# Moving high halves behind the next exponential, and four other steps, in a transformer block with adaptive LayerNorm

## The chip, the cores and the metric

The kernel runs on one core of one Trainium2 chip. The metric is the device time of one execution in microseconds; the time before is the median of three runs.

## The reference

One transformer block on 2048 tokens of 512 features, in float32. `c` is a vector of 512 numbers, from which six vectors of 512 follow (shift, scale and gate for each half of the block). The key and value caches are cut to their last 512 positions, without a mask; 32 query heads share 8 key heads of 128 features.

```python
mod = (_silu(c) @ w_mod).reshape(1, 6, 1, -1)          # sa, ca, ga, sb, cb, gb
h = layernorm(x) * (1 + ca) + sa
q = (h @ wq).reshape(1, 2048, 32, 128)                  # heads first
p = softmax(q @ k.T * 128 ** -0.5)                      # 512 keys
x = x + ga * ((p @ v) @ wo)                             # wo: 4096 x 512
h = layernorm(x) * (1 + cb) + sb
x = x + gb * ((gelu(h @ w_gate) * (h @ w_up)) @ w_down) # 512 x 1792 twice, 1792 x 512
```

## The kernel before

**Halves.** Each float32 operand of a matmul is split into a high half in float16 and a low half, the rest, also in float16. A product takes three matmuls of 128x128 by 128x512: high by low, high by high, low by high (`mm3`, L87 to L91). For scores the order is q's high half with K's low half, q's high with K's high, and then q's **low** half with K's high. `split_post` (L746 to L748) makes the halves of a product or of loaded weights: ScalarE (ACT) writes the high half, scaled, and a function that is returned writes the low half later on VectorE (DVE).

**Units and slots.** The attention has 128 units: a head and 512 tokens each. A unit has four slots of 128 tokens, so there are 512 slots (T = 512); unit u has slots 4u to 4u+3. A slot t issues, in this order (the loop begins at L1564): the scores of t on TensorE (PE) into one of two PSUM banks; the maximum `nm` of the row on DVE (L990); the entries noted for ("e", t), which are low halves of q and of outputs; the low half of p for slot t-3 on DVE (L1016) and its DMA transpose on SyncE (SP, L1020); the entries ("d", t), other work of DVE; the exponential of t on ACT (L999), which frees the scores' bank, and in odd slots the row sums' copy (L1004); the high half of p for slot t-2 on ACT (L1011); the entries ("x", t); then three products from a list (`pop`): q of the next unit, p times v of unit u-2, and the output projection; then loads, and the entries ("w", t). Nothing is reordered after that: each engine takes its instructions in the order in which the slots issue them. `at(key, fn)` notes an entry, `soon(fn)` notes it for ("d", now+1), `first(fn)` for ("e", now+1).

**The first three groups** (units 0 to 11) compute q directly (`q_plain`); from unit 12 on, 2x2 Strassen products with seven instead of eight blocks do it, two heads and 1024 tokens at a time. For unit u of the first kind q is complete after the second slot of the unit before, 4u-3, and `q_post` (L760) then issues its high half on ACT at once, ahead of the exponential of slot 4u-2; the low half follows in ("e", 4u-2). Weights of q for group 2 (`plain_steps`, L836 on) are split in slots 19 and 21, K of group 2 (`k_items`) in slot 24, each with its high half at the end of the slot and the low half in ("d", t+1).

**Combinations.** The Strassen products need sums of four blocks of LayerNorm output (b11, y, b22, b21), which lie in DRAM ("hs"). `combos` (L570 on) loads them ("cb") and issues differences on GpSimd (POOL, L582), high halves on ACT (L380) and low halves on POOL (L384). In the attention `sched_combos` (L1182 on) puts them at slots: for gen 1 from slots 201 and 234 on, for gen 2 (the feed-forward part of the first 1024 tokens) from 478 and 488 on. A load goes out `ahead` slots before the first use of its tile, 3 everywhere (`AHEAD`). The last ones (gen 3) are placed by hand in the feed-forward part by steps: step q is product q % 7 of group q // 7.

**LayerNorm of gen 2.** When the last projection of a tile of 128 tokens is added up (`attn_final`, L966 on), seven steps of its second LayerNorm are noted for later slots: statistics, normalising on POOL, the turn (four PE transposes into a PSUM bank `pln`, L508), two halves of scale and shift on ACT into `hf` (L516), after the second of which SP stores the tile to "hs", and two splits. Tiles 0 to 7 are concerned. PSUM banks "acc" are five in rotation, shared by q, p times v, projections, the turn and others.

**The feed-forward part** also uses Strassen products; the third product is transposed (`yt_tasks`, L1687) and DVE multiplies gate by up (L1294).

Of the kernel before, what the change touches and what calls it, by code (L numbers as in the profile page):

```python
# [26 lines left out]
QT = QB // P  # L27
EPS = 1e-5
SCALE = DH ** -0.5
AHEAD = 3  # L30
# [35 lines left out]
def block_kernel(ctx: ExitStack, tc: tile.TileContext, x, kT, v, wq, wo, wg, wu, wd, cT, wc, wm, out):  # L66
    nc = tc.nc
# [10 lines left out]
    def raw(name):  # L78
        return pool.tile([P, 512], F32, tag="raw", name=name, bufs=NRAW)
# [15 lines left out]
    def dma(out_, in_):  # L95
        moved[0] += 1
        nc.sync.dma_start(out_, in_)
# [81 lines left out]
    def col(name, i=0):  # L179
        return ST[name][:, i:i + 1]  # L180
# [193 lines left out]
    def stored(gen, name, p):  # L374
        qb, dt = {"b11": (0, p), "b21": (0, 2 + p), "y": (1, p), "b22": (1, 2 + p)}.get(name, (None, None))
        return spilled(gen, name)[:, p, :] if qb is None else spilled(gen, qb)[:, dt, :]

    def put(gen, name, p, src, eng):
        def high():
            nc.scalar.activation(block(gen, name)[:, p, :], src(), AF.Copy)  # L380

        def low():
            t = block(gen, name)
            eng.tensor_tensor(t[:, 2 + p, :], src(), t[:, p, :], op=ALU.subtract)  # L384

        return high, low
# [183 lines left out]
    def combos(gen, p, eng, base=True, d=0, e=0):  # L570
        X = {}

        def load(name):
            if gen == 0 and (p == 0 or name in ("b21", "b22")):
                X[name] = kept({"b11": "s1", "y": "u2", "b21": "u3"}[name]) if name != "b22" else \
                    pool.tile([P, 512], F32, tag="w2", name="cb", bufs=2)
            else:
                X[name] = raw("cb")
            dma(X[name], stored(gen, name, p))

        def diff(o, a, b):
            return lambda: nc.gpsimd.tensor_tensor(X[o], X[a], X[b], op=ALU.subtract)  # L582

        def parts(pos, name, tile_):
            high, low = put(gen, name, p, lambda: X[tile_], eng)
            return [(pos, high), (pos + 1 + e, low)]

        def plain(pos, name):
            return parts(pos, name, name) if base else []

        return [
            (lambda: load("b11"), plain(0, "b11") + [(2, diff("b11", "y", "b11"))] + parts(d + 4, "t1", "b11")),
            (lambda: load("y"), [(2, nop), (3, diff("y", "b22", "y"))] + parts(d + 5, "t3", "y")),
            (lambda: load("b22"), (plain(1, "b22") or [(2, nop)]) + [(4, diff("b22", "b22", "b11"))] + parts(d + 6, "t2", "b22")),
            (lambda: load("b21"), plain(3, "b21") + [(5, diff("b21", "b21", "b22"))] + parts(d + 7, "t4", "b21")),
        ]
# [15 lines left out]
    qT, pT, oT, E = {}, {}, {}, {}  # L612
# [3 lines left out]
    def sched(pos, ld, *more, kind="raw", ahead=AHEAD):  # L616
        loads.append(((pos,) + more, ld, kind, ahead))
# [10 lines left out]
    def get_qt():  # L628
        return pair("qt", "qt", 3)
# [106 lines left out]
    now = [0]  # L736
    later = {}

    def at(key, *fns):
        later.setdefault(key, []).extend(fns)  # L740
# [5 lines left out]
    def split_post(t, src, scale):  # L746
        nc.scalar.activation(t[:, 0, :], src, AF.Copy, scale=scale)  # L747
        return lambda: nc.vector.scalar_tensor_tensor(t[:, 1, :], src, scale, t[:, 0, :], op0=ALU.mult, op1=ALU.subtract)  # L748

    def soon(*fns):  # L750
        at(("d", now[0] + 1), *fns)

    def first(*fns):

        at(("e", now[0] + 1), *fns)

    def q_scale(u):
        return col("qsc", units[u][1])

    def q_post(u, ps):  # L760
        qT[u] = get_qt()
        first(split_post(qT[u], ps, q_scale(u)))

    def q_sum(u, t, ps, dst):
# [23 lines left out]
    SET, RAW = {}, {}  # L788
# [47 lines left out]
    def plain_steps(key, by):  # L836
        def part(k):
            SET.setdefault(key, [None, None])[k] = get_w(k)
            if key > 1:
                return soon(split_post(SET[key][k], RAW[key][k], by))  # L840
            times(RAW[key][k], by)
            halves(SET[key][k], RAW[key][k])

        return lambda: part(0), lambda: part(1)
# [50 lines left out]
    def kept(k):  # L895
        return pool.tile([P, QB], F32, tag=k, name=k, bufs=1)
# [69 lines left out]
    def attn_final(ti):  # L966
        y1[ti] = dram.tile([P, D], F32, name=f"y{ti}")
        dma(y1[ti], acc[ti])
        if ti < 2 * QT:
            nxt = ti + 2 * QT  # L970
            own, steps = ln_tile(2, ti, lambda: acc[ti])
            own()
            for d, fn in zip((1, 5, 8, 9, 10, 12, 13), steps):
                at(("w", now[0] + d), fn)
            at(now[0] + 12, lambda: load_acc(nxt, rows_of(x, nxt)))
        else:
            ln_last(ti - 2 * QT)
# [204 lines left out]
    def sched_combos(gen, p, base):  # L1182
        for k, (load, steps) in enumerate(combos(gen, p, nc.gpsimd if gen or p == 0 else nc.vector, False, 0 if gen else 1 if p else 2, 0 if gen or p else 5)):
            if gen == 0 and (p == 0 or k > 1):
                at(base + ((0, 0, 0, 2)[k] if p else (-10, -2, -1, -9)[k]), load)
                for off, fn in steps:
                    at(("w", base + off), fn)
            else:
                sched(base + steps[0][0], (load, [fn for _, fn in steps]), *[base + off for off, _ in steps[1:]])

    for p in range(2):
        sched_combos(0, p, CB[p])
# [25 lines left out]
    for g in range(NG):  # L1218
        half, pr = divmod(g, NPR)
        t0 = 16 * g  # L1220
        qd = pr // 2
        srcs = [wq[2 * pr], wq[2 * pr + 1]]
        by = col("wsc", pr)
        spread = None if half else lambda m, pr=pr: w_spread(pr, m)
        if 0 < g < GW:
            a, b = plain_steps(g, by)
            sched_pair(g, srcs, t0 - (19 if g > 1 else 13), spread, [(t0 - (13 if g > 1 else 8), a)], [(t0 - (11 if g > 1 else 7), b)])
        elif g >= GW and (not half or pr < GW):
            sched_set(g, srcs, t0, by, spread)
            if not half:  # L1230
                a, b, c, d, e, f = SETPOS2 if g == GW else SETPOS
                for k, pos in ((0, t0 - b + 4), (3, t0 - c + 4), (1, t0 - e + 4), (2, t0 - f + 4)):
                    at(pos, lambda g=g, k=k: store_set(g, k))
        elif half:
            for k, hi in ((0, 15), (1, 10), (2, 9), (3, 7)):
                within(t0 - 18, t0 - hi, lambda g=g, pr=pr, k=k: set_fetch(g, pr, k))
        if half:
            within(t0 - 14, t0 - 5, lambda pr=pr: k_fetch(pr))
            if pr % 2 == 0:
                within(t0 - 6, t0 + 3, lambda qd=qd: v_fetch(qd))  # L1240
                for k in range(4):
                    within(t0 + 4 + 2 * k, t0 + 22 + 2 * k, lambda h=4 * qd + k: wo_fetch(h))
        else:
            if g > 0:
                if pr % 2 == 0:
                    load, stat, spread_, parts = k_items(pr)
                    sched(t0 - (22 if g > 2 else 20), (load, [stat]))
                    at(("w", t0 - (19 if g > 2 else 17)), spread_)
                load, stat, spread_, parts = k_items(pr)
                sched(t0 - (7 if g > 2 else 8 if g > 1 else 6), (load, [parts if g != 2 else lambda parts=parts: soon(parts(True))]))  # L1250
                at(t0 - (3 if g > 2 else 1 if g > 1 else 2), lambda pr=pr: store(("k", pr), KV[0, pr, 0]))
                if pr % 2 == 0:
                    load, stat, spread_, parts = v_items(qd)
                    sched(t0 + 1, (load, [stat, spread_, parts]), t0 + 3, t0 + (6 if g > 2 else 5))
                    at(t0 + 10, lambda qd=qd: store(("v", qd), KV[0, qd, 1]))
            if pr % 2 == 0:
                wo_items(qd, [t0 + o + (qd == 7) for o in WOS[min(qd, 2)]], [t0 + o for o in WOP[min(qd, 2) + qd // 6]])
# [303 lines left out]
    with tc.manual_schedule():  # L1561
        begin()
        nexty, invs = [], {}
        for t in range(T + TAIL):  # L1564
            now[0] = t
            u, s = divmod(t, 4)
# [80 lines left out]
    def step(q, fn):  # L1647
        f_at(q // 7, q % 7, fn)

    for i, q in enumerate((16, 19, 22, 26, 30, 33, 36, 40)):  # L1650
        load, norm, split, turn = ln_turned(i)
# [3 lines left out]
        step(q + 4, turn)  # L1655
    for q, (qb, dt) in zip((37, 41, 44, 47, 50, 51, 54, 55), ((0, 0), (0, 2), (0, 1), (0, 3), (1, 0), (1, 2), (1, 1), (1, 3))):
        step(q, lambda qb=qb, dt=dt: turned_out(qb, dt))
    for p, (q, at_) in enumerate(((59, (61, 62, 62, 63, 64, 65, 66, 67, 68)), (70, (75, 76, 76, 79, 80, 81, 82, 89, 90)))):
        for load, steps in combos(3, p, nc.gpsimd):
            step(q, load)  # L1660
            for off, fn in steps:
                step(at_[off], fn)

    def whole(ti):
        if ti in halfway and ti in joined:
# [174 lines left out]
```

## Time and profile before

| | us |
|---|---|
| median of three runs (1731.09 to 1735.14) | 1733.09 |
| the profiled execution | 1734.19 |
| its span, first to last instruction | 1732.4 |
| TensorE busy | 1711.2 |
| VectorE busy | 1425.8 |
| ScalarE busy | 1254.3 |
| GpSimd busy | 1093.3 |

The profile is one execution. Its page gives the busy time of each engine and the costliest groups of instructions; other views of the same trace give waits (who waited for whom, us in total, times, longest), stretches of time, and the order of time: start, duration, engine, line, operation, output <- inputs, form, count, and in brackets the idle time of that engine before it with what ended it. A wait is put down to what came last by the profile, which need not be what was waited for. PE's instructions overlap: a row's end is later than the next row's start.

### The profile page before, as it was taken

How to read it: one execution, taken by the hardware profiler on the slowest of the kernel's cores; microseconds unless marked ns; L12 is line 12 of the kernel's file. 1: busy time of each engine (PE TensorE's matmuls, PEld its weight loads, DVE VectorE, ACT ScalarE, POOL GpSimd, SP SyncE). 2: the span in 40 equal slices, each digit the busy share in tenths (PEclk: the TensorE clock that was granted, in tenths of full speed). 3: DMA queues.
4: the chain of work that ended last, by engine and by line, in shares of the span. 5: the costliest groups of instructions: out<-in, count | busy, mean ns of one | idle time of the engine just before them, and what ended most of it. 6: DMA issues, size and time to landing. Idle time of an engine off the chain costs nothing.

```text
span 1732.4 us, 26343 instructions
## 1 busy us (share of the span) xinstructions
PE 1711.2 (99%) x8012; PEld 787.1 (45%) x8012; DVE 1425.8 (82%) x2476; ACT 1254.3 (72%) x2819; POOL 1093.3 (63%) x1328
## 2 busy tenths in 40 slices
PE   7999999999999999999999999999999999999998
PEld 5444444444444444444444444444444444444444
DVE  7888898988888899888888888888896788676666
ACT  6988788888888777897787777787785354455442
POOL 4879778777788884655665755747760345735424
PEclk9999999999999999999999999999999999999999
DMA  7999999999999998999999999999997556355353
GB/s 234 218 208 210 214 214 205 225 205 220 211 229 222 206 210 181 219 207 224 198 232 219 206 231 208 203 218 221 229 227 164 163 145 196 118 164 174 96 157 104
DMA packets 693454, 343.51 MB, mean 198 GB/s; under 512 B 579136, under 2 KB 602688, under 8 KB 693312
## 3 DMA queue, kind: packets, MB, share of 16 engines
q1 hardware_dynamic: 693024, 341.30, 85.4%
q8 instruction: 63, 1.03, 0.3%
q14 instruction: 79, 0.65, 0.1%
q10 hardware_dynamic: 288, 0.52, 0.1%
HBM read 137.50 MB, written 63.70 MB: 116 GB/s over the span
## 4 chain that ended last, share of the span: by engine, by line
PE 86%; DVE 5%; ACT 4%; POOL 2%; DMA 2%; issue 1%; SPq 0%; POOLq 0%; DVEq 0%; ACTq 0%
PE py L91 18%; PE po L91 17%; PE ps L91 16%; PE fa L91 8%; PE qa L91 8%; PE fc L91 4%; PE qc L91 4%; PE ya L91 3%; PE fb L91 2%; PE qb L91 2%; PE yc L91 2%; ACT ee L999 1%; DVE p L1016 1%; DVE nm L990 1%; ACT p L1011 1%
## 5 line engine op out<-in xcount | busy, mean ns | idle before, releaser
L999 ACT ACTIVATE ee<-ps,nm 128x512 f32<-128x512 f32 x512 | 349.6, 683 | 184.2 <-DVE nm L990 181.0
L1016 DVE SCALAR_TENSOR_TENSOR p<-ee,rr,p 128x512 f16<-128x512 f32 x512 | 454.1, 887 | 8.1 <-ACT p L1011 7.5
L990 DVE TENSOR_REDUCE nm<-ps 128x1 f32<-128x512 f32 x512 | 350.3, 684 | 105.7 <-PE ps L91 102.9
L91 PE MATMUL ps<-k,qt 128*128 128x512 f16 x1536 | 414.9, 379 | 3.8 <-ACT ee L999 2.5
L1011 ACT ACTIVATE p<-ee,rr 128x512 f16<-128x512 f32 x512 | 363.9, 711 | 21.9 <-DMA pt<-p 11.6
L91 PE MATMUL po<-pt,v 128*128 128x512 f16 x1536 | 372.9, 379 | 2.8 <-DVE kmax L184 1.0
L91 PE MATMUL py<-wo,ot 128*128 128x512 f16 x1536 | 371.3, 379 | 0.0
L91 PEld LDWEIGHTS <-w 128*128 128x128 f16 x2184 | 214.0, 98 | 259.7 <-issue 2.7
L91 PEld LDWEIGHTS <-v 128*128 128x128 f16 x1536 | 149.9, 98 | 185.1 <-issue 5.1
L91 PEld LDWEIGHTS <-ot 128*128 128x128 f16 x1536 | 150.3, 98 | 181.2
L91 PEld LDWEIGHTS <-qt 128*128 128x128 f16 x1536 | 145.8, 98 | 174.8 <-issue 3.3
L1320 POOL TENSOR_TENSOR fg<-fg 128x512 f32<-128x512 f32 x48 | 63.0, 1312 | 147.0 <-DVE fg L1294 144.2
L748 DVE SCALAR_TENSOR_TENSOR ot<-po,ot 128x512 f16<-128x512 f32 x128 | 87.8, 686 | 37.7 <-ACT ot L747 37.3
L1304 ACT ACTIVATE at<-fg 128x512 f16<-128x512 f32 x92 | 56.3, 626 | 80.1 <-DVE fg L1294 61.7
L999 ACT ACTIVATION_READ_ACCUMULATOR ee<-ps,nm 128x1 f32 x512 | 100.1, 195 | 0.0
L960 DVE SCALAR_TENSOR_TENSOR acc<-py,ysc,acc 128x512 f32<-128x512 f32 x128 | 94.7, 740 | 5.3 <-PE py L91 5.3
L91 PE MATMUL qa<-t,w 128*128 128x512 f16 x348 | 84.9, 379 | 0.0
L236 POOL TENSOR_TENSOR lw<-lw,half__86 128x1 f32<-128x1 f32 x39 | 25.0, 641 | 91.0 <-DVE lw L186 91.0
L91 PE MATMUL fa<-t,w 128*128 128x512 f16 x336 | 81.7, 379 | 0.1
L747 ACT ACTIVATE ot<-po 128x512 f16<-128x512 f32 x128 | 73.9, 577 | 5.0 <-PE po L91 5.0
L403 POOL TENSOR_TENSOR rs<-rs,nhalf 128x1 f32<-128x1 f32 x32 | 18.7, 586 | 92.9 <-DVE rs L397 90.0
L91 PEld LDWEIGHTS <-wo 128*128 128x128 f16 x504 | 49.3, 98 | 60.6 <-issue 1.3
(243 smaller groups left out, 2821.9 us busy)
## 6 DMA issues: line engine op xcount, KB each, us to landing
w<-kept SPq DMA_DIRECT2D x123, 256.0 KB, 3.3
wo<-kept SPq DMA_DIRECT2D x72, 256.0 KB, 3.3
kept<-stage SPq DMA_DIRECT2D x67, 256.0 KB, 3.2
raw<-in_wo SPq DMA_DIRECT2D x56, 256.0 KB, 3.2
kept<-w SPq DMA_DIRECT2D x39, 256.0 KB, 3.3
rw<-in_wq SPq DMA_DIRECT2D x38, 256.0 KB, 3.1
hs<-hf SPq DMA_DIRECT2D x32, 256.0 KB, 2.8
pt<-p SPq DMA_TRANSPOSE x512, 3.5
```

The source lines that it names most:

```text
L91: nc.tensor.matmul(ps, a, b, start=first and n == 0, stop=last and n == 2, skip_group_check=chain)
L236: nc.gpsimd.tensor_tensor(out, out, half_, op=ALU.pow)
L403: nc.gpsimd.tensor_tensor(st["rs"], st["rs"], nhalf, op=ALU.pow)
L747: nc.scalar.activation(t[:, 0, :], src, AF.Copy, scale=scale)
L748: return lambda: nc.vector.scalar_tensor_tensor(t[:, 1, :], src, scale, t[:, 0, :], op0=ALU.mult, op1=ALU.subtract)
L960: nc.vector.scalar_tensor_tensor(acc[ti], st["p"], by, acc[ti], op0=ALU.mult, op1=ALU.add)
L990: nc.vector.tensor_reduce(nm, E[t]["ps"], axis=AX.X, op=ALU.max, negate=True)
L999: nc.scalar.activation(e, E[t]["ps"], AF.Exp, bias=E[t]["nm"], scale=1.0, accum_out=sm[:, t % 2:t % 2 + 1])
L1011: nc.scalar.activation(p16[:, 0, :], E[t]["e"], AF.Copy, scale=E[t]["r"])
L1016: nc.vector.scalar_tensor_tensor(p16[:, 1, :], E[t]["e"], E[t]["r"], p16[:, 0, :], op0=ALU.mult, op1=ALU.subtract)
L1304: nc.scalar.activation(t[:, 0, :], g, AF.Copy)
L1320: nc.gpsimd.tensor_tensor(g[o], g[a], g[b], op=ALU.subtract)
```

## The change

Five edits. First, for units 3 to 7 the high half of q is issued one slot later, after that slot's exponential and high half of p, and its low half one slot later too. Second, the same for the weights of group 2 and for K of group 2. Third, the loads of combinations of gen 1 and gen 2 go out 3, 2, 1 and 3 slots ahead instead of 3 each: b11, y and b22 no longer in the same slot. Fourth, for tiles 3 and 7 the turn and the four steps after it come one slot later. Fifth, in the last combinations (second half of gen 3) the difference `y` goes from step 79 to 81, `b22` from 80 to 82, `b21` from 81 to 89, and the high and low halves that need them are spread over steps 83 to 96 (before: 81 to 90).

```diff
     def q_post(u, ps):
         qT[u] = get_qt()
+        if 2 < u < 8:
+            return at(("x", now[0] + 1), lambda: first(split_post(qT[u], ps, q_scale(u))))
         first(split_post(qT[u], ps, q_scale(u)))
...
             if key > 1:
-                return soon(split_post(SET[key][k], RAW[key][k], by))
+                return at(("x", now[0] + 1), lambda: soon(split_post(SET[key][k], RAW[key][k], by)))
...
-            for d, fn in zip((1, 5, 8, 9, 10, 12, 13), steps):
+            for d, fn in zip((1, 5, 9, 10, 11, 13, 14) if ti % QT == QT - 1 else (1, 5, 8, 9, 10, 12, 13), steps):
                 at(("w", now[0] + d), fn)
...
-                sched(base + steps[0][0], (load, [fn for _, fn in steps]), *[base + off for off, _ in steps[1:]])
+                sched(base + steps[0][0], (load, [fn for _, fn in steps]), *[base + off for off, _ in steps[1:]], ahead=(3, 2, 1, 3)[k] if gen else AHEAD)
...
-                sched(t0 - (7 if g > 2 else 8 if g > 1 else 6), (load, [parts if g != 2 else lambda parts=parts: soon(parts(True))]))
+                sched(t0 - (7 if g > 2 else 8 if g > 1 else 6), (load, [parts if g != 2 else lambda parts=parts: at(("x", now[0] + 1), lambda: soon(parts(True)))]))
...
-    for p, (q, at_) in enumerate(((59, (61, 62, 62, 63, 64, 65, 66, 67, 68)), (70, (75, 76, 76, 79, 80, 81, 82, 89, 90)))):
-        for load, steps in combos(3, p, nc.gpsimd):
-            step(q, load)
-            for off, fn in steps:
-                step(at_[off], fn)
+    for load, steps in combos(3, 0, nc.gpsimd):
+        step(59, load)
+        for off, fn in steps:
+            step((61, 62, 62, 63, 64, 65, 66, 67, 68)[off], fn)
+    for (load, steps), at_ in zip(combos(3, 1, nc.gpsimd), ((75, 76, 76, 80, 81), (76, 81, 83, 89), (76, 76, 82, 88, 89), (79, 80, 89, 95, 96))):
+        step(70, load)
+        for (_, fn), k in zip(steps, at_):
+            step(k, fn)
```

## Prediction

> **What bounds the kernel now.** I read the page first, then who waited for whom on PE, then the order of time around each wait.
>
> ```profile
> span 1732.4 us, 26343 instructions
> ...
> PE 1711.2 (99%) x8012; PEld 787.1 (45%) x8012; DVE 1425.8 (82%) x2476; ACT 1254.3 (72%) x2819; POOL 1093.3 (63%) x1328
> ...
> L91 PE MATMUL ps<-k,qt 128*128 128x512 f16 x1536 | 414.9, 379 | 3.8 <-ACT ee L999 2.5
> ```
>
> TensorE is busy for 99% of the span (the last row is one group: the scores, 379 ns each, 3.8 us of idle time before them), and no edit here removes or adds a matmul. So the change can only move the few places where PE stands still. In slots 15 to 31 of the attention this is its longest wait, by the view of waits cut to 62 to 98 us (total, times, longest):
>
> ```profile
> PE ps L91 <- ACT ee L999: 2.4, 3, 1.9
> ```
>
> The scores of a slot (ps) wait for the exponential two slots earlier, since there are two banks for scores. The longest, 1.9, is before the scores of slot 24. In order of time:
>
> ```profile
> 80.81 0.68 ACT L747 ACTIVATE qt<-pq,qsc 128x512 f16<-128x512 f32 x1
> 81.39 0.72 ACT L747 ACTIVATE w<-rw,wsc 128x512 f16<-128x512 f32 x1
> 81.53 0.75 DVE L748 SCALAR_TENSOR_TENSOR qt<-pq,qsc,qt 128x512 f16<-128x512 f32 x1 [0.98 <-ACT qt L747]
> 82.00 0.66 ACT L999 ACTIVATE ee<-ps,nm 128x512 f32<-128x512 f32 x1
> 82.66 0.69 ACT L1011 ACTIVATE p<-ee,rr 128x512 f16<-128x512 f32 x1
> 82.82 0.95 PE L91 MATMUL ps<-k,qt 128*128 128x512 f16 x3 [1.86 <-ACT ee L999]
> ```
>
> The exponential of slot 22 (82.00) stands on ACT behind the high half of q for unit 6 (80.81) and behind a high half of the weights (81.39). Both are what the first two edits move. After that wait the granted clock is low for one window (0.52, third from the right, in the table by stretches):
>
> ```profile
> 83.20:86.60 3.40, 3.40 (x10) 1.21 (x9) 3.40 (x7) 2.44 (x7) 3.22 (x4) 0.52 1.17 303
> ```
>
> At clock 0.52 this stretch lost 3.40 x 0.48 = 1.6 us of matmul time.
>
> **The change part by part.** Durations are from the profiled execution: 1734.19 us, span 1732.4, so 1.8 us around it.
>
> *High halves in slots 9 to 26.* No instruction is added. What is moved: for units 3 to 7 the high half of q goes from the end of slot 4u-3 to after the exponential **and** after the high half of p of slot 4u-2; the low half follows a slot later. But the scores of slot 4u need this q. So q's high half, which lay one slot ahead of need, becomes the last thing before them. Take unit 4:
>
> ```profile
> 62.39 0.68 ACT L747 ACTIVATE qt<-pq,qsc 128x512 f16<-128x512 f32 x1
> 62.96 0.63 ACT L219 ACTIVATE junk<-rw 128x512 f16<-128x512 f32 x1
> 63.58 0.66 ACT L999 ACTIVATE ee<-ps,nm 128x512 f32<-128x512 f32 x1
> ...
> 64.41 0.82 PE L91 MATMUL ps<-k,qt 128*128 128x512 f16 x3
> ```
>
> Now: q, statistics, exponential 14 until 64.24, scores of 16 at 64.41. After: all moves forward by q's 0.57 (62.39 to 62.96), but behind the exponential come the high half of p and that of q, 0.69 (row 82.66) and 0.68, or 0.6 each without the 0.1 by which such rows overlap. The scores can begin at 64.41 - 0.57 + 1.2 = 65.04. Their third matmul, 2 x 0.22 after the first (0.22 is (0.82 - 0.38) / 2, with the 0.38 of one alone), reads q's low half, 0.75 on DVE (row 81.53): it starts at 65.8 instead of 64.85, **0.95 later**. The same sum holds for units 5, 6 and 7. For slot 24 (unit 6) the exponential comes earlier by q and the weights ahead of it (0.58 + 0.61), and then p's and q's halves come behind it, 1.2: nothing gained there either.
>
> These delays don't add up, though, because ACT is the pace here: PE waits for it three times anyway, 2.4 us in all, and a delay of PE before slot 24 comes off the 1.86 us there. What ACT itself stood still is the bound of any gain. The two rows are the waits of ACT from 60 to 98 us and the busy time of PE, weight loads, DVE, ACT and POOL there:
>
> ```profile
> ACT ee L999 <- DVE nm L990: 1.9, 3, 0.9
> ...
> 60.00:98.00 38.00, 34.67 (x151) 14.94 (x152) 32.91 (x59) 35.58 (x88) 29.69 (x37) 0.96 1.03 221
> ```
>
> ACT is busy for 35.58 of the 38 us, longer than PE. What stays is what happens at the last deferred q, unit 7, after which PE sets the pace again:
>
> ```profile
> 88.11 0.72 ACT L747 ACTIVATE k<-raw,ksc 128x512 f16<-128x512 f32 x1
> 90.82 0.68 ACT L747 ACTIVATE qt<-pq,qsc 128x512 f16<-128x512 f32 x1
> 91.39 0.66 ACT L999 ACTIVATE ee<-ps,nm 128x512 f32<-128x512 f32 x1
> ...
> 90.61 0.68 DVE L990 TENSOR_REDUCE nm<-ps 128x1 f32<-128x512 f32 x1
> 91.53 0.75 DVE L748 SCALAR_TENSOR_TENSOR qt<-pq,qsc,qt 128x512 f16<-128x512 f32 x1 [0.24 <-ACT qt L747]
> ...
> 91.63 1.46 PE L91 MATMUL ps<-k,qt 128*128 128x512 f16 x6
> 97.06 0.59 PE L91 MATMUL po<-pt,v 128*128 128x512 f16 x2 [0.61 <-DVE nm L990]
> ```
>
> The six matmuls at 91.63 are slots 27 and 28 without a gap; slot 28 begins at 92.28. Also, since exponential 26 ends at 92.05, it could not have begun earlier: so the 1.6 us of slow clock before it cost this kernel at most 0.2 us, and nothing is won where it goes. After: K's high half (0.72) leaves slot 24 and lands before exponential 26, q's leaves that place; nm of slot 26 is ready at 91.29; the exponential stays at about 91.3 to 91.9, p's half until 92.6, q until 93.2, the third matmul 0.75 later at 94.0 instead of 92.85: 1.15 late. Against that the product po waits 0.61 at 97.06. I read this as the transposed p of slot 23, whose low half now no longer stands behind q's low half on DVE (0.75, row 91.53): the wait goes. Net **+0.5**. Bounds: everything that ACT and po waited comes back, -1.9 - 0.6 = -2.5; four delays in full, 4 x 1.05 = +4.2. I take +0.5, since it follows from rows at the place where PE takes over the pace. The weights' own move costs nothing: they are first read in slot 28, K in slot 32, and their low halves end by about 87 and 93; if that cover were gone, it would be their 0.75 on DVE once each. The raw tiles that the low halves free are loaded anew only some us later. On DVE the low half of p, and so its transpose, is queued behind each low half that waits.
>
> *Combination loads.*
>
> ```profile
> 535.92 1.48 SPq L97 DMA_DIRECT2D cb<-hs  x3
> 537.49 1.49 SPq L1020 DMA_TRANSPOSE pt<-p  x1
> 540.28 3.52 SPq L1020 DMA_TRANSPOSE pt<-p  x1
> ...
> 547.28 1.89 PE L91 MATMUL po<-pt,v 128*128 128x512 f16 x8 [1.01 <-DVE kmax L184]
> ```
>
> Three loads of 256 KB go out in one slot ahead of two transposes; the second of them needs 3.52 us to be issued, and po then waits 1.01. After, the second load is issued one slot and the third two slots later, behind one transpose each, so the third no longer stands before the transpose at 540.28. POOL takes each tile two slots after its new issue, some 5 us; if that were too little, POOL's differences would wait, and no matmul of these slots reads them. I take **-1.0**; between 0 (wait only moved) and -1.0. The other three groups of such loads (slots 233, 477, 487) lie where the view of PE's waits shows none: 0.
>
> *LayerNorm turn of tiles 3 and 7.*
>
> ```profile
> 730.70 0.80 ACT L516 ACTIVATE hf<-pln,cols 128x128 f32<-128x128 f32 x2
> 731.65 0.52 PE L508 MATMUL pln<-ident,acc 128*128 128x128 f32 x3 [0.63 <-POOL w L159]
> 774.51 0.63 PE L508 MATMUL pln<-ident,acc 128*128 128x128 f32 x4 [0.32 <-ACT hf L516]
> ```
>
> The view names POOL for the first, but the bank is what the tile before freed at 731.50, when its last hf ended. One slot later the bank is long free: **-0.63** for tile 3; its store on SP passes one transpose, and no wait of PE follows for 40 us. For tile 7 the 0.32 goes too, but every later step of that tile moves with it, its store on SP among them:
>
> ```profile
> 784.63 0.55 SPq L97 DMA_DIRECT2D hs<-hf  x1
> 789.49 0.36 SPq L97 DMA_DIRECT2D rw<-in_wu  x1
> 789.90 0.52 SPq L97 DMA_DIRECT2D kept<-stage  x1
> 790.53 1.32 SPq L1020 DMA_TRANSPOSE pt<-p  x1
> ...
> 794.47 1.89 PE L91 MATMUL po<-pt,v 128*128 128x512 f16 x8 [0.55 <-DMA pt<-p]
> ```
>
> One slot on, the store of 784.63 stands behind the next transpose and behind that slot's load and store (789.49, 789.90), right ahead of the transpose at 790.53, for which po waits. The load at 789.49 waits for a tile that POOL frees, so it comes no earlier. The transpose moves by the store's 0.55 and the 0.32 is waited for here instead: **+0.55** on this stretch, between -0.32 (the store is hidden) and +0.9 (its transfer delays the transpose's as well).
>
> *Last combinations.*
>
> ```profile
> 1485.00 2.61 POOL L582 TENSOR_TENSOR cb<-cb 128x512 f32<-128x512 f32 x2
> 1486.36 1.81 DVE L1294 SCALAR_TENSOR_TENSOR fg<-fg,gsc,fu 128x512 f32<-128x512 f32 x1
> 1493.76 0.81 DVE L1294 SCALAR_TENSOR_TENSOR fg<-fg,gsc,u 128x512 f32<-128x512 f32 x1
> 1489.53 0.81 PE L91 MATMUL ya<-at,wo 128*128 128x512 f16 x3 [0.77 <-DVE yt L1687]
> ```
>
> Beside POOL's two differences the DVE product takes 1.81 us; its like at 1493.76 takes 0.81. The two differences go two steps later, so the product ends some 1.0 us sooner, and with it the addition yt, for whose bank ya waits: the 0.77 goes: **-0.77**. No DMA is moved here. The same POOL work comes at steps 81 to 96, ahead of the first use at step 98: between -0.77 and, if one such product is slowed there in turn, +0.2.
>
> Sum: 0.5 - 1.0 - 0.63 + 0.55 - 0.77 = **-1.35**, hence 1732.85 for such an execution. The profiled one lay 1.10 above the median of the runs, 1733.09; taken from that median, **1731.7**.
>
> **The rivals.**
>
> *The slots gain as meant.* ACT makes good all that it waited: -2.5 in place of +0.5, the others as they are with tile 7 at 0: -2.5 - 1.0 - 0.63 - 0.77 = -4.9, **1728.2**. For it: the one long wait names ACT, and the two rows ahead of its exponential are the ones that go. Against: ACT is full there; moving work within a full engine frees none of it.
>
> *The wait for q takes the place of the wait for the exponential, in all four units* (slots 16, 20, 24, 28). That is slower than before. Price 4.2, and one stretch at half clock more, 1.6; less 1.85 for the other three parts: +3.95, **1737.0**. It decides on whether ACT runs on while PE waits: if the maxima that ACT needs come late because the scores came late, each delay is carried on.
>
> *Only the clock.* The new wait before slot 28 is about 1.6 us with two matmuls and then half a us more, like the one that brought 0.52 at 83.20; this time no wait of ACT's follows that would swallow the loss. +1.6: **1733.3**. [...]
>
> *The change doesn't do what it says*: the waits at 547, 731 and 1489 only turn up a little later. Then +0.5 alone: **1733.6**.
>
> **How the numbers follow.** Forecast 0.42 (1731.7, give or take 1.5), gain as meant 0.22, clock 0.14, nothing 0.08, q in all units 0.14. A measurement of this kernel can tell about 0.2%, 3.5 us, from no change: faster means under 1729.6, slower above 1736.6. Faster: most of the second case and a little of the first, 0.24. Slower: most of the last, 0.12. Same: 0.64. The range takes in the second case down to 1727.5 and the bounds of the first and the clock's case up to 1736.0; outside lies the last case and a little below, under 0.2.
>
> **What would show it.** Right: scores of slots 16, 20, 24 and 28 waiting for "ACT qt" or "DVE qt" in place of "ACT ee"; no wait of po near 547, of pln near 731 and of ya near 1489; po near 794 waiting longer for its transpose. Wrong: scores of slot 24 or 28 beginning earlier against the slots before them than now, or new waits of PE beyond slot 32 in the attention.

## The result and the profile after

The changed kernel takes 1735.63 us (median of 22 runs, 1733.86 to 1737.38), the kernel before 1733.01 (22 runs): a ratio of 1.0015, 95% interval 1.0009 to 1.0021. So it is slower, by 2.6 us, where 1.35 us less was forecast. The profiled execution took 1736.34 us, against 1734.19 before. One of the 11 executions of the kernel without the slots' edits, further below, took 7384 us; it moves the median there by less than 0.1.

The page of the changed kernel, first lines and the group of the scores:

```profile
span 1734.6 us, 26346 instructions
...
PE 1710.8 (99%) x8010; PEld 786.4 (45%) x8012; DVE 1422.2 (82%) x2476; ACT 1254.4 (72%) x2819; POOL 1094.3 (63%) x1328
...
L91 PE MATMUL ps<-k,qt 128*128 128x512 f16 x1536 | 415.9, 379 | 8.8 <-ACT qt L747 5.6
```

The work is the same; what grew is idle time ahead of the scores, 3.8 to 8.8 us, and q is now its main cause. To place the loss I set the start of each slot's scores beside its start in the trace of before (each start counted from the first instruction of its trace). After minus before, in us:

| slot (time before) | 30 (98) | 207 (549) | 280 (735) | 283 (743) | 296 (778) | 303 (796) | 511 | last matmul |
|---|---|---|---|---|---|---|---|---|
| late by | +1.47 | +1.14 | +0.31 | +0.85 | +0.34 | +3.52 | +2.94 | +2.14 |

The steps between the columns belong to one edit each: the high halves +1.5; the loads -0.3; tile 3's turn -0.8, then +0.5 at tile 4; tile 7's turn -0.5 for its own bank, then +3.2; the last combinations -0.9 (between 511 and the end, where smaller steps of both signs come to +0.1). The -0.6 between slots 303 and 511 is of no edit: most of it, at slots 459 to 462, is there with q's move alone too. The loss is made in two places.

**Slots 15 to 31.** Waits of PE from 62 to 98 us in the changed kernel (total, times, longest):

```profile
PE ps L91 <- ACT qt L747: 4.4, 4, 1.4
PE po L91 <- DVE p L1018: 1.0, 1, 1.0
PE ps L91 <- DVE qt L748: 0.7, 4, 0.2
```

The four waits for q are those that were foretold, and no wait for the exponential is left. The second row was not foretold. In order of time:

```profile
85.34 0.74 DVE L1018 SCALAR_TENSOR_TENSOR p<-ee,rr,p 128x512 f16<-128x512 f32 x1
...
86.00 1.70 DVE L748 SCALAR_TENSOR_TENSOR w<-rw,wsc,w 128x512 f16<-128x512 f32 x1
86.61 0.81 PE L91 MATMUL ps<-k,qt 128*128 128x512 f16 x3
87.24 0.94 POOL L159 TENSOR_SCALAR wo<-wor 128x512 f16<-128x512 f32 x1
87.63 0.68 DVE L992 TENSOR_REDUCE nm<-ps 128x1 f32<-128x512 f32 x1
88.34 0.66 ACT L1001 ACTIVATE ee<-ps,nm 128x512 f32<-128x512 f32 x1 [1.54 <-DVE nm L992]
89.08 1.46 PE L91 MATMUL po<-pt,v 128*128 128x512 f16 x6 [1.00 <-DVE p L1018]
```

A low half of the weights, 1.70 us on DVE (86.00), now stands ahead of a maximum, that of slot 24 (87.63). Behind that maximum the exponential waits 1.54 on ACT, and the transposed p comes 1.00 late for po.

**Tile 7.** Waits of PE from 722 to 800 us:

```profile
PE ps L91 <- ACT ee L1001: 2.0, 1, 2.0
PE pln L508 <- ACT hf L516: 0.3, 1, 0.3
```

Neither the old wait of pln at 774 nor that of po at 794 is there. The first row is new, and it is ACT's, not SP's:

```profile
777.80 3.80 POOL L1381 TENSOR_TENSOR rw<-rw 128x256 f32<-128x256 f32 x4
...
785.65 0.67 POOL L530 TENSOR_TENSOR b<-hf,b 128x256 f16<-128x256 f32 x1
...
780.18 0.71 ACT L1013 ACTIVATE p<-ee,rr 128x512 f16<-128x512 f32 x1
786.35 0.81 ACT L516 ACTIVATE hf<-pln,cols 128x128 f32<-128x128 f32 x2 [5.46 <-POOL b L530]
787.05 0.68 ACT L1001 ACTIVATE ee<-ps,nm 128x512 f32<-128x512 f32 x1
...
787.88 0.81 PE L91 MATMUL ps<-k,qt 128*128 128x512 f16 x3 [2.04 <-ACT ee L1001]
788.52 3.77 PE L91 MATMUL po<-pt,v 128*128 128x512 f16 x9
```

ACT stands still for 5.46 us at its first write of tile 7's `hf`, with exponentials queued behind it, until POOL's last read of tile 6's `hf` (785.65). That read waits its turn on POOL behind eight microseconds of other work. Then nine matmuls take 3.77 us. Two stretches with the granted clock (third column from the right):

```profile
784.00:788.00 4.00, 1.96 (x10) 0.83 (x9) 0.62 (x1) 1.62 (x6) 2.23 (x3) 1.00 0.80 181
788.00:792.00 4.00, 4.00 (x12) 1.45 (x11) 2.67 (x5) 3.83 (x10) 0.00 (x0) 0.60 0.77 178
```

The cause lies in the buffers. `hf` is taken from `raw`, five buffers (L78), which it shares with the staging of the feed-forward weights (`stage`). Which of the five a request gets stands in the addresses of the built programs. In the kernel before, tile 7's `hf` has the buffer that tile 5's had; in the changed kernel it has the very buffer of tile 6's, and its first write waits for POOL's read of that. The order of the requests is the same in both: tile 7's comes right after tile 6's. But one slot later it comes behind the issue of tile 6's last read on POOL, in the same slot 296; before, it came in slot 295, ahead of that read. With tile 7's turn alone moved, the addresses change in this way; with tile 3's alone they don't. By which rule the build picks a buffer is not shown here.

### The profile page after: what moved, and what is told of

Same layout as the page of the kernel before. It is cut to its first block, busy times and chain, and to the rows that moved or that the text cites. A ratio compares the mean times of both kernels' runs of the same rounds, so it can differ in the third digit from the quotient of the medians.

```text
span 1734.6 us, 26346 instructions
## 1 busy us (share of the span) xinstructions
PE 1710.8 (99%) x8010; PEld 786.4 (45%) x8012; DVE 1422.2 (82%) x2476; ACT 1254.4 (72%) x2819; POOL 1094.3 (63%) x1328
## 4 chain that ended last, share of the span: by engine, by line
PE 90%; DVE 3%; ACT 2%; POOL 2%; DMA 1%; issue 1%; SPq 0%; POOLq 0%; ACTq 0%; DVEq 0%
PE py L91 19%; PE po L91 18%; PE ps L91 17%; PE fa L91 8%; PE qa L91 8%; PE fc L91 4%; PE qc L91 4%; PE ya L91 3%; PE fb L91 2%; PE qb L91 2%; PE yc L91 2%; PE pq L91 1%; PE yb L91 1%; DVE nm L992 1%; ACT ee L1001 1%
```

## The experiments

My theory after the two traces: the slots lose because of the weights' low half on DVE besides the foretold half microsecond for q, and tile 7 loses because of the buffer that it gets from `raw`; the other edits gain. The rivals: q's waits carry the whole of the slots' loss; tile 7's wait belongs to SP or to what came before it. All times are medians of 11 runs, beside runs of the kernel before on the same chip; the ratio is taken over all of them and is not that of the two medians.

| kernel | us | before there | ratio, 95% interval |
|---|---|---|---|
| slots alone | 1735.07 | 1733.29 | 1.0008, 1.0 to 1.0017 |
| q alone | 1732.95 | 1733.29 | 0.9997, 0.9988 to 1.0006 |
| q and K | 1733.25 | 1733.38 | 1.0001, 0.9992 to 1.001 |
| weights alone | 1732.95 | 1733.38 | 0.9997, 0.9988 to 1.0006 |
| loads alone | 1732.54 | 1733.38 | 0.9995, 0.9986 to 1.0004 |
| turns alone | 1734.9 | 1733.38 | 1.0008, 0.9999 to 1.0017 |
| last combinations alone | 1733.04 | 1733.38 | 0.9998, 0.9989 to 1.0006 |
| all but the slots | 1734.09 | 1733.29 | 1.0003, 0.9994 to 1.0012 |
| all, own buffer for tile 7 | 1732.5 | 1733.29 | 0.9995, 0.9987 to 1.0004 |
| mended | 1730.2 | 1733.38 | 0.9983, 0.9974 to 0.9992 |
| mended, tile 4 later too | 1729.95 | 1733.38 | 0.9981, 0.9972 to 0.9989 |

Most single intervals take in 1, and each reaches about 1.5 us to either side, so the places and sizes below are read from the traces, one execution of each kernel. The medians agree with them, but can't prove them: slots +1.8, turns +1.5, loads -0.8, last combinations -0.3 make +2.2, beside the 2.6 measured for all.

**The slots: all three, all but the three, q alone.** The first has the edits of `q_post`, of the weights and of K on the kernel before; the second is the changed kernel without these; the third has only this:

```diff
     def q_post(u, ps):
         qT[u] = get_qt()
+        if 2 < u < 8:
+            return at(("x", now[0] + 1), lambda: first(split_post(qT[u], ps, q_scale(u))))
```

> The kernel before with the first two edits alone (high halves of q, of the weights and of K one slot later). Theory A (the loss has two sources, the slots and the turn of tile 7): the scores of slots 16, 20, 24 and 28 wait for q as in the changed kernel, the product of slot 25 waits 1.0 us for DVE, PE is 1.5 us late at slot 30 and stays so: 1734.5 us, +1.5 on before. Rival B (the slots carry the whole loss): +2.6 or more, 1735.6. Rival C (the slots cost nothing in the end): 1733.0.

> The changed kernel with the first two edits undone: loads, LayerNorm turns and last combinations are as changed. Theory A: PE is where it was in before at slot 30, loses 2.7 us between slots 295 and 303, gains 0.3 at slot 206, 0.3 at slots 278 to 283 and 0.9 in the last combinations: about +1.2 on before, 1734.1 us. Rival B (the loss is all in the slots): 1731 to 1731.5.

> The kernel before with the deferral of q alone; weights and K as before. Theory A (of the slots' loss about 1 us is the weights' low half, which on DVE came ahead of the maxima of slot 24, and 0.5 the wait for q before slot 28): the waits for q at slots 16, 20, 24, 28 are there, no wait of PE for DVE before slot 26, PE about 0.5 late at slot 30: 1733.5 us. Rival B (q's waits carry the slots' whole loss): PE 1.5 late at slot 30, 1734.5.

Measured: with all three, slot 30 is 1.35 late where slot 0 was 0.20 early, so the slots cost 1.55. With q alone slot 30 is 0.10 late and slot 0 0.34 early: 0.44, with the same four waits and without the wait of po at 97.06. That is the +0.5 of the prediction, for q. About 1.1 remains for weights and K. Without all three, slot 30 stands where it stood in before (0.03 late against slot 0), and the time is 1734.09, as the theory has it: the slots carry part of the loss, not the whole.

**Which of the two, and alone or together.** `qk_only` leaves the weights where they were; `w_only` moves nothing else:

```diff
             if key > 1:
-                return soon(split_post(SET[key][k], RAW[key][k], by))
+                return at(("x", now[0] + 1), lambda: soon(split_post(SET[key][k], RAW[key][k], by)))
```

> The kernel before with the moves of q's and K's high halves alone; the weights' stand where they stood. Theory (the weights' low half on DVE, moved ahead of the maxima of slot 24, is the part of the slots' cost that q alone does not bring): scores of slot 30 about 0.45 us late against before, as in the kernel with q's move alone, no wait of about 1.0 us of the product po for DVE in slot 25 or 26; span like that kernel's, about 1731.7, time about 1733.5. Rival (K's move brings it): scores of slot 30 about 1.5 us late and the wait of po there, span 1733.2.

> The kernel before with the move of the weights' high halves alone. Theory (a low half of the weights, 1.2 to 1.7 us on DVE beside POOL, falls ahead of the maxima of slot 24 once it is a slot later, whether q moves or not): the product po of slot 25 or 26 waits for DVE and slot 30 is 0.5 to 1.1 us late; about 1734. Rival (it costs only where q's waits have pushed everything back): slot 30 level with before or, with the high half out of the exponential's way before slot 24, up to 0.6 earlier.

Waits of PE from 62 to 98 us, first with q and K moved, then with the weights alone:

```profile
PE ps L91 <- ACT qt L747: 3.8, 4, 1.3
PE ps L91 <- DVE qt L748: 0.7, 4, 0.2
```

```profile
PE ps L91 <- ACT ee L999: 2.1, 3, 1.3
PE po L91 <- DVE p L1016: 1.2, 1, 1.2
PE po L91 <- DVE nm L990: 0.7, 1, 0.7
```

Without the weights' move there is no wait of po for DVE: that wait is theirs. Slot 30 then is 0.53 late and slot 0 0.29 early, 0.82 in all, 0.4 more than with q alone. This 0.4 is not K's. It is there at slot 16 already (1.29 late against slot 0, with q alone 0.89), and K's halves are moved in slot 24. It comes in at slot 14, where kernels that have no edit so early differ as well: the one with the turns alone loses 0.46 there on before, the one with the last combinations alone gains 0.21. From slot 16 to slot 30, q and K together win back 0.47 and q alone 0.45, while with the weights too 0.66 is lost, and 0.69 in the changed kernel. So K costs nothing, as the theory had it, and the weights 1.1. But with the weights alone the wait of po is there, 1.2 us, and slot 30 is 0.47 **early**, slot 0 0.18 early: a gain of 0.3. The rival of that run was right. Moving the weights also shortens the wait ahead of the scores of slot 24, 1.86 before and 1.32 here, and what po loses is made good by slot 30. Behind q's delays it is all loss; that this is because the scores of slot 24 are late there already is how I read it, not shown. So the 1.1 is an effect of the two edits together, not of either.

**Tile 7: a buffer of its own; the turns alone.**

```diff
-                st["f"] = raw("hf") if gen == 2 else tmp("hf")
+                st["f"] = pool.tile([P, 512], F32, tag="hf7", name="hf", bufs=1) if gen == 2 and qb and i == QT - 1 else raw("hf") if gen == 2 else tmp("hf")
```

> The changed kernel, with a buffer of its own for tile 7's hf, which otherwise takes the fifth buffer after tile 6's in the raw rotation. Theory A (ACT's hf waits 5.46 us until POOL has read tile 6's hf from the buffer that tile 7 is to get, and PE waits 2.0 us for the exponential behind it, then runs a window at half clock): ACT's wait, PE's wait before slot 299 and the half clock go, PE gains about 2.7 us between slots 295 and 303: 1732.9 us. Rival B (the store of tile 7 ahead of a transpose on SP, as I predicted, is what costs): PE still waits near 790 to 797, for the transpose, and gains less than 0.5: 1735.2 or more.

> The kernel before with the later turn of tiles 3 and 7 alone. Theory: tile 3 -0.8 near 732 and +0.5 near 743, tile 7 -0.5 for its own wait and then the wait of about 2.0 for the exponential near 788 that its hf brings: between +1.3 and, with the clock at half behind that wait, +3.0; about 1735. Rival (the wait for hf only came with another edit): no wait of PE near 788, 0.6 less than before.

One thing in the first of these is not so: tile 7 has tile 6's buffer, but not because it comes fifth after it in a rotation (see above).

With the changed kernel otherwise as it is, the buffer takes away ACT's wait, PE's wait and the low clock. ACT's first write of tile 7's `hf`, and the two stretches:

```profile
781.30 0.80 ACT L516 ACTIVATE hf<-pln,cols 128x128 f32<-128x128 f32 x2
...
784.00:788.00 4.00, 4.00 (x20) 1.85 (x19) 3.50 (x6) 3.37 (x9) 3.20 (x4) 1.00 0.79 186
788.00:792.00 4.00, 4.00 (x20) 1.77 (x19) 3.89 (x7) 3.97 (x12) 0.67 (x1) 1.00 1.23 234
```

From slot 296 to slot 303 it gains 0.70 on before where the changed kernel loses 3.18, and the time falls from 2.6 us above the kernel before to 0.8 below it. The store on SP, the only cost the prediction had here, has no effect: the view of PE's waits from 722 to 800 has a single row, that of pln at tile 4. The turns alone bring the same wait without any other edit, with the clock full behind it (waits and a stretch of that kernel):

```profile
786.28 0.81 PE L91 MATMUL ps<-k,qt 128*128 128x512 f16 x3 [1.99 <-ACT ee L999]
```

```profile
788.00:792.00 4.00, 3.96 (x19) 1.76 (x18) 3.84 (x8) 3.80 (x10) 0.00 (x0) 1.00 0.67 155
```

There slots 296 to 303 lose 1.64, in the kernel without the slots' edits 1.67; so the low clock made up some 1.5 of the 3.18 in the profiled execution of the changed kernel (3.18 less the 1.65 without it). How often it falls in its other executions the runs don't say.

**Loads alone.** The edit of `sched_combos` on the kernel before, nothing else.

> The kernel before with the changed lead of the combination loads alone. Theory: the wait of po near 547 us (1.01 before) goes, down to between nothing and 0.66, and nothing else of PE changes: 0.4 to 1.1 us less than before, about 1732.5. Rival (the wait is only moved to where the later loads stand ahead of a transpose): PE is level with before by slot 212, 1733.2.

PE has no wait at all from 530 to 560 us; slot 207 is 1.34 early, slot 0 0.14 early: a gain of 1.2, as foretold. In the trace of the changed kernel 0.66 of the wait stays, though its loads have the same leads. Its SP queue, and POOL:

```profile
538.00 1.28 SPq L1022 DMA_TRANSPOSE pt<-p  x1
539.33 2.33 SPq L97 DMA_DIRECT2D cb<-hs  x2
...
545.12 2.34 SPq L1022 DMA_TRANSPOSE pt<-p  x1
...
546.71 1.32 POOL L582 TENSOR_TENSOR cb<-cb 128x512 f32<-128x512 f32 x1 [2.94 <-DMA cb<-hs]
...
548.40 2.12 PE L91 MATMUL po<-pt,v 128*128 128x512 f16 x9 [0.66 <-DMA pt<-p]
```

Two things here are not as the prediction has them. The first load does not stay in its slot: the planner behind `sched_combos` lets loads out in the order of their uses, so b11 with its lead of 3 is queued behind y with its lead of 2, and the two go out together (x2), a slot later. And POOL's difference then waits 2.94 for its data. But the 0.66 belongs to this one execution. The kernel with tile 7's own buffer has the same instructions up to there; in its trace the like of the transpose at 545.12 takes 1.28 us in place of 2.34, PE has no wait from 530 to 560 us, and slots 205 to 207 gain 1.16 (1.17 without the slots' edits, 0.33 in the changed kernel):

```profile
545.85 1.28 SPq L1022 DMA_TRANSPOSE pt<-p  x1
```

Why it took longer in the one execution stays open.

**Last combinations alone.**

> The kernel before with the last combinations at their later steps alone. Theory (DVE's product near 1487 no longer runs beside POOL's two differences): product 0.75 in place of 1.81, no wait of ya, -0.8 to -0.9 in the profile. Two kernels with the old steps had the short product as well, by what stood in the tenths of a microsecond of their order, so the mean over runs should gain less than that: 0.3 to 0.9, about 1732.8. Rival (a later product is slowed in its turn): level with before.

The product takes 0.75 us and ya doesn't wait. Over the runs the median gains 0.3, and the interval takes in both nothing and the 0.9 of the trace. That the gain can't be had in every execution is shown by the traces of other kernels, with the **old** steps. The kernel with the turns alone, then the one with the loads alone:

```profile
1485.56 3.20 POOL L582 TENSOR_TENSOR cb<-cb 128x512 f32<-128x512 f32 x2
...
1486.87 0.75 DVE L1294 SCALAR_TENSOR_TENSOR fg<-fg,gsc,fu 128x512 f32<-128x512 f32 x1
```

```profile
1484.46 2.61 POOL L582 TENSOR_TENSOR cb<-cb 128x512 f32<-128x512 f32 x2
...
1485.78 1.83 DVE L1294 SCALAR_TENSOR_TENSOR fg<-fg,gsc,fu 128x512 f32<-128x512 f32 x1
```

In the first the product begins 1.31 us after POOL's pair and has 0.75, and POOL's pair takes 3.20 in place of 2.61; in the second it begins 1.32 after and has 1.83. In the first it is POOL's pair that takes longer, in the second DVE's product. Of seven profiled executions with the old steps three paid the wait of ya (before, slots alone, loads alone; 1.32 to 1.38 us after) and four did not (1.23 to 1.31). The 0.77 was a property of the one execution that I read.

**Mended.** The changed kernel without the slots' edits, with tile 7's buffer, and with leads by which y and b11 go out in their queue's order, a slot apart:

```diff
+                sched(base + steps[0][0], (load, [fn for _, fn in steps]), *[base + off for off, _ in steps[1:]], ahead=(2, 3, 1, 3)[k] if gen else AHEAD)
```

The second has the later turn for tile 4 too: `if ti in (3, 4, 7)`.

> The changed kernel without the moves of the high halves, with the leads of the combination loads in the order that keeps the first two a slot apart, and with tile 7's hf in a buffer of its own; the two turns and the last combinations as in the changed kernel. Theory (each part's own gain stands once its side effect is gone): loads -1.1, tile 3 -0.8 and +0.5 back at tile 4, tile 7 -1.2, last combinations -0.9: 3.5 less than before, about 1729.7. Rival (a wait comes back elsewhere, behind transposes or at the bank of tile 4 above all): 1732 to 1733.

> The same with the later turn for tile 4 as well. Theory (tile 4's pln waits for the last hf of tile 3, which now comes a slot later): its wait of 0.34 to 0.5 us near 743 goes, 0.5 us less than without, about 1729.2. Rival (the wait goes on to tile 5, whose turn is the early one): level with the kernel without it.

Both are faster than the kernel before, 1730.2 and 1729.95 us, and so than the changed one. Waits of PE from 722 to 800 us, the first kernel, then the second:

```profile
PE pln L508 <- ACT hf L516: 0.3, 1, 0.3
```

```profile
PE ps L91 <- DMA k<-kept: 0.5, 1, 0.5
```

Tile 4's wait for tile 3's last `hf` goes with the later turn, as the theory has it, but some 50 us on PE waits for a load of K, as it does not in the first: 0.4 gained at slot 283, 0.7 given back at slot 304. The two are level.

## Why the prediction was wrong, step by step

- **Slots, +0.5; measured +1.5.** For q the step was right: the four waits, their place, the vanished wait at 97.06, and 0.44 measured alone. Failed: "The weights' own move costs nothing". I looked at who needs the weights (slot 28) and not at what stands behind their low half on DVE, the maximum of slot 24; and the three moves were summed as if each met the kernel before, while the weights' costs 1.1, and only behind q's. K's was rightly put at nothing. Of the rivals, the gain as meant did not come, and the one that pays each of the four waits for q in full (4.2) is refuted by q alone.
- **Clock.** Foretold: nothing is won where the slow stretch at 83.20 goes. The four kernels with the old order whose clock stayed full there begin slot 25 some 1.5 us earlier than before and slot 30 from 0.0 to 0.3 later, each less its offset at slot 0: right. The rival in which the new wait before slot 28 halves the clock did not come: 1.00 from 60 to 98 us in the changed kernel.
- **Loads, -1.0; -1.2 in three traces, -0.3 in that of the changed kernel.** Right in size, but for that one execution; wrong in which loads move, since the order of the planner's queue was not read.
- **Tile 3, -0.63; -0.8 at its place, +0.5 back at tile 4.** The bank that came free late for tile 3 now does so for tile 4, which waits 0.34 at 743.29. The prediction looked for a wait "for 40 us" on the strength of SP alone.
- **Tile 7, +0.55; measured +2.7.** The sign was right for a wrong reason. This is the step that failed most: SP's queue was followed, the buffer that the moved step asks for was not: it brought PE a wait of 2.0, behind 5.46 us in which ACT stood still, and in this execution some 1.5 more by the low clock, while the store on SP cost nothing.
- **Last combinations, -0.77; -0.9 in the trace, -0.3 by the medians, which is not clear of noise.** Right in the product (0.75 us in place of 1.81) and in ya, but the cost stood in only some executions of the old steps.

With the measured sizes of the slots (1.0 more) and of tile 7 (2.1 more) -1.35 becomes +1.7, with tile 4's wait (0.5) and the loads in this execution (0.7 less gain) +2.9; the larger gains of tile 3 (0.2) and the last combinations (0.1) and the half microsecond that no edit touches bring it to the +2.1 between the spans.

## What to carry to other kernels

When a step is moved, follow each buffer that it takes from a shared set, and see whose last read it now waits for and on which queue that read stands; a move by one slot can make a step wait for a queue that it never touched, as ACT did here for 5.46 us. Ask of moved work what is behind it on its engine, not only who needs it (here a low half of 1.70 us stood on DVE ahead of a maximum, and the exponential behind that waited 1.54), and price moves together where the first shifts the place of the second. Before you count a wait as a gain, look whether other executions have it: with DVE's product 1.31 us behind POOL's pair the 0.8 us was not there at all, with 1.32 it was. When two traces are set side by side, take the offset right ahead of the edit, not at the start: 0.4 us that came before K's move looked like its cost.

## What the runs showed of the hardware

**The same wait came with full clock and with half.** The wait before slot 24 is 1.86 us in seven kernels with the old order. With the last combinations alone, and then with the loads alone (order of time, then the stretch behind it):

```profile
82.49 0.81 PE L91 MATMUL ps<-k,qt 128*128 128x512 f16 x3 [1.86 <-ACT ee L999]
```

```profile
83.20:86.60 3.40, 3.38 (x16) 1.37 (x15) 3.40 (x7) 2.44 (x8) 3.22 (x4) 1.00 1.09 276
```

```profile
82.67 1.11 PE L91 MATMUL ps<-k,qt 128*128 128x512 f16 x3 [1.86 <-ACT ee L999]
```

```profile
83.20:86.60 3.40, 3.40 (x10) 1.25 (x9) 3.40 (x7) 2.45 (x6) 3.23 (x4) 0.52 1.04 277
```

Behind the same wait the clock was full in four of the seven profiled executions and half (0.50 to 0.52 over 3.4 us) in three. Behind the wait at tile 7 it was 0.60 over 4 us in the changed kernel (2.04 us of wait) and 1.00 with the turns alone (1.99). In the five kernels with the moved q, whose waits for it in slots 16 to 28 are 0.8 to 1.4 us, it is 1.00 from 60 to 98 us throughout.

The clock records of two traces say more. Ahead of the last matmuls the trace of before has one half-speed stretch, the one behind the 1.86 us, and that of the changed kernel has one, at tile 7. Each lasts 3.413 us; they begin 64.853 and 771.412 us after the execution's first record of full clock, which is 19.0 and 226.0 times 3.413. In the 3.41 us right ahead PE was busy 39% of the time in the one (1.34 of 3.42) and 40% in the other (1.37 of 3.41), the least of all stretches of 3.413 us counted from that first record. The stretch ahead in the kernel before (full clock still), then the same place in the first mended kernel, where the clock stayed full (mean of that execution 1.0):

```profile
79.94:83.36 3.42, 1.34 (x6) 0.57 (x6) 2.44 (x6) 3.39 (x10) 3.24 (x4) 1.00 1.26 112
```

```profile
79.84:83.25 3.41, 1.55 (x8) 0.60 (x7) 2.43 (x5) 3.41 (x8) 3.14 (x5) 1.00 0.95 133
```

The stretch ahead and the slow one in the kernel with tile 7's own buffer:

```profile
22.91:26.33 3.42, 1.90 (x7) 0.34 (x5) 3.04 (x7) 2.18 (x5) 1.19 (x2) 1.00 0.97 319
26.30:29.75 3.45, 3.22 (x8) 1.19 (x9) 2.65 (x8) 2.11 (x4) 1.11 (x2) 0.51 0.50 162
```

No limit follows from these: behind a stretch with PE busy for 45% (1.55 of 3.41) the clock was full, behind one with 56% (1.90 of 3.42) it was half. What decides is not shown.

**A DVE product beside POOL's differences: one of the two took longer.** In the seven profiled executions with the old steps POOL's pair took 3.12 to 3.20 us beside a product of 0.75 where the product began 1.23 to 1.31 us after the pair (four executions), and 2.61 beside a product of 1.78 to 1.83 where it began 1.32 to 1.38 after (three). That is 0.5 to 0.6 us more for POOL or 1.0 to 1.1 for DVE. What lies behind it is not shown.
